# Single-tile groups at both ends of a fused block's second part, and a new planned order

## The chip, the cores and the metric

The kernel runs on one core of a Trainium2 chip. The core has five engines that work in parallel, each on its own queue of instructions in a fixed order: TensorE (PE in the profile, with its weight loads as PEld), VectorE (DVE), ScalarE (ACT), GpSimd (POOL) and SyncE (SP, which here only starts transfers). The metric is device time in microseconds, lower is better; before and after are compared by the medians of repeated runs on the same chip.

## What is computed

One block of a network on 2048 positions and 640 channels, in bfloat16. First a mixer: a short and a long convolution over positions (the long one as a Fourier transform of length 4096), gated by a normalized copy of the input. Then an MLP with a shift of channel groups along the positions. Six modulation vectors come from `c`.

```python
mod = (_silu(c) @ w_mod).reshape(c.shape[0], 6, 1, -1)     # sa, ca, ga, sb, cb, gb
h = _layernorm(x) * (1 + ca) + sa
x = x + ga * _A_ref(h, A_k, A_v, A_shift_k, A_ssm_k, A_ssm_D)
h = _layernorm(x) * (1 + cb) + sb
x = x + gb * _B_ref(h, B_w1, B_w2, B_w3, B_w4)

def _A_ref(q, k, v, shift_k, ssm_k, ssm_D):
    ...                                   # k_shift: 4-tap convolution of k
    kv = k_shift * v
    ...                                   # y: kv convolved with ssm_k, by FFT
    return q * (y + kv * ssm_D)

def _B_ref(x, w1, w2, w3, w4):
    h = _gelu(_layernorm(x) @ w1)         # w1: 640 x 640
    ...                                   # four groups of channels shifted by +1, -1, +2, -2
    x1 = x + hs                           # hs = shifted h @ w2, 640 x 640
    return x1 + _gelu(_layernorm(x1) @ w3) @ w4   # w3: 640 x 1728, w4: 1728 x 640
```

## The kernel before

The 2048 positions are 16 tiles of 128. The first part does the transforms: `stage1` and `stage2` for the filter and for the product k_shift * v, then `inverse1` (ten blocks of spectral products, `TA` and `TB` on DVE at L605, each with a half-swap of the filter's spectrum by two DMAs, L601, one from SP and one from POOL) and `inverse2` (L657, 512 small matmuls in six groups of tiles). In the first part DVE and ACT mostly evict PSUM (L208, L210). The modulation vectors (`mod_half`, L482) are made beside it.

The second part goes tile by tile through a long chain:

- `chain_a`: gate and first residual (L714, L717, with the row sum as a by-product), the sum of squares on ACT (`square_sum`, L706), `ln_finish` (mean, variance, root);
- `chain_b`: norm (L580 on ACT or L582 on DVE), times 1 + cb (L728), plus sb (L729), squares, `ln_finish`;
- `chain_c`: norm and `turn`, which transposes the tile, on PE (L747, with a copy at L753 or L755) for the first groups, by a DMA of SP (L740) for the rest;
- `mm_w1`: W1 and its GELU (L794, L796 and, for the fifth block of channels, L804, L810). The shift by one or two positions is a shift of 32 or 64 columns in the buffer `gsf`, as positions are strewn over tiles; at the first and last tile small copies (L817 to L833) make the wrap-around;
- `mm_w2`: W2 (L849), second residual (L857), squares, `ln_finish`, norm and `turn`;
- `mm_w3`: W3 in four pieces (named f0, f4, f8, f12 below) and GELU (L882, L886);
- `mm_w4`: W4 (L928, and L934 for the last half block), final residual (L951, L956, L957) and the stores. The last tile has its own ending, `last_tile`.

`ln_finish` (L687) makes, for a group of two tiles, the negative mean and the part of the variance that comes from it on POOL or DVE (L692 to L694), then on POOL the variance, its power -0.5 and the product of the two (L699, L700, L701).

All of it is done in pairs of tiles: `chain_a` to `mm_w1` for tiles (0, 1), (2, 3) and so on, `mm_w2` to `mm_w4` for (1, 2), (3, 4) up to (15, 0). `spare` adds, in four groups of `mm_w4`, a DVE transpose (L896 to L902) and a POOL operation (L908 to L914) on a buffer that is no longer used.

The order of the work is not left to the program's loops. Each step is a task with a number, an engine, and its reads and writes; the string `ORDER` at the top lists the tasks in the order in which they are issued, with the engine and the PSUM places chosen. It was made beforehand by a planner that works with the costs in the `add` calls; the kernel only replays it. So each engine runs its tasks in the order of the string.

Of the kernel before, what the change touches and what calls it, by code (L numbers as in the profile page):

```python
# [16 lines left out]
P = 128  # L17
# [9 lines left out]
0S 18D 2S 19G 36G 56G 21G 20D 23D 24A 22D 25A 27G 28D 29D 31A 37G 68G 69D 30A 32D 26G 84P:0 85A 90P:1 88P:2 91A 89A 4S 72G 73D 106P:3 107A 3S 70G 50G  # L27
71D 102P:0 103D 38G 39G 104P:1 105A 6S 86P:2 87D 40A 49G 96P:3 97A 92P:0 93A 94P:1 8S 118P:2 5S 74G 95A 75D 1S 66G 98P:3 99A 41G 112P:0 113A 116P:1 9S
119D 67D 114P:2 108P:3 42G 43G 51D 44A 53A 117D 115A 10S 122P:0 110P:1 52D 11S 123D 109A 34S 100P:2 101D 54A 33S 57G 82P:3 78P:0 79D 201S 111A 45G 83A
55G 80P:1 76P:2 253D 47S 120P:3 81A 77A 170P:0 171A 121D 46S 194P:1 195A 178P:2 179A 198P:0 35S 144P:1 145A 199D 142P:3 143D 188P:2 189A 176P:0 177D  # L30
202S 182P:1 183A 48S 140P:3 141A 180P:2 181D 148P:0 149A 156P:1 164P:3 165A 157D 138P:2 139D 190P:0 136P:1 137D 191A 162P:3 163A 200S 174P:2 175A 12S
172P:0 173D 196P:1 197A 152P:3 153D 13S 160P:2 203S 168P:0 169D 7S 146P:1 161A 147A 186P:3 187D 154P:2 166P:0 155A 167D 58G 59G 192P:1 193A 150P:3
151A 60A 61G 258P:2 158P:0 159A 254D 184P:1 185A 259D 213A 208A 126P:3 127D 272P:0 273A 266P:1 267D 124P:2 125D 270P:3 271A 209D 214A 14S 130P:1
262P:2 263A 65G 219S 220P:0 221A 255D 15S 128P:3 16S 131D 260P:2 129D 17S 62G 63G 64A 222S 261A 264P:0 265A 211A 210D 256D 132P:1 274P:3 275A 276P:2
277A 225S 134P:0 133D 268P:3 269A 135D 223P:1 224A 288P:2 289A 212G 489D 280P:0 281A 282P:3 283A 226P:1 284P:2 257D 290P:0 227D 291A 228S 285D 231S
234S 205S 286P:1 287D 278P:3 279A 480D 292P:2 232P:0 251G 296P:1 293A 233D 252S 294P:3 247G 486D 297D 229P:0 230D 235P:2 236D 362S 295A 298P:3 299A
249G 316P:1 360P:0 317D 361A 304P:2 305D 350P:3 351A 346P:1 347A 300P:0 301D 332P:2 333A 238G 354P:3 355D 312P:1 313A 302P:0 303D 340P:2 341A 243S
318P:3 319D 358P:1 359A 336P:0 337A 386S 342P:2 248G 308P:3 343D 237S 310P:1 244S 311D 330P:0 309A 331A 352P:2 353D 314P:3 315A 306P:1 322P:0 323A
326P:2 327A 334P:3 307D 335D 338P:1 339A 250G 320P:0 324P:2 325A 344P:3 242G 348P:1 349A 321D 328P:0 245S 241G 240S 356P:2 345D 329D 357A 364D 363G
365D 366P:3 367A 370S 368P:1 481D 239S 246G 372D 369A 371G 387G 373D 374P:0 375A 376P:2 377A 216A 378S 380D 379G 381D 442S 443P:3 382P:1 395G 383A  # L40
384P:0 389D 385A 388D 394S 397D 396D 392P:2 483A 393A 390P:1 404D 215G 398P:0 400P:2 401A 399A 403G 402S 405D 444D 408P:3 412D 406P:2 445S 409A 407A
411G 410S 413D 416P:0 417A 419G 414P:3 415A 446P:2 420D 418S 421D 422P:0 454S 424P:3 428D 427G 391A 426S 435G 429D 423A 434S 455P:1 456A 436D 432P:0
433A 447D 437D 430P:1 431A 451S 452P:2 487D 453A 490D 491D 438P:0 440P:1 439A 457S 458P:2 441A 459A 448S 449P:0 450A 425D 501G 217D 479G 492D 475S
493D 484D 485D 482D 495P:31 496A 497A 519D 520D 218G 522D 498P:20 523D 473S 499D 204S 500A 521A 525G 488D 474S 543D 476S 524A 557D 526G 554D 558D
502P:31 504A 503A 555D 531D 559A 556A 508P:02 509A 510A 511P:13 544D 532D 494D 527D 528D 533D 534A 529D 530A 505P:02 513A 206S 512A 560G 561G 566A
562D 602D 535G 536G 545D 605D 477S 563D 606D 540D 541P:3 472S 537D 607A 538P:1 603D 539D 567D 568D 542A 478G 551P:3 546D 564D 608G 604A 609G 610D 207S
578A 570D 506D 514S 549P:1 569A 565A 571G 572D 575D 611D 552A 614A 573P:0 574D 576P:3 577D 586P:0 550A 615D 584P:1 616D 617A 612D 613A 553G 587A 618D
619G 579D 580D 547D 515S 548D 672D 585A 620D 621P:3 623D 624P:0 625A 675D 676D 677A 591P:1 673D 674A 678G 592D 588P:0 622A 634P:3 632P:1 679G 680D
589D 593A 635A 684D 685D 681D 682D 686D 688D 594G 590A 633A 595G 596D 599D 636P:0 637D 518G 600P:3 597P:1 601D 598D 507A 639P:2 656P:0 463A 687A 640D
642D 683A 638A 689G 690D 692A 641A 643G 657A 693S 461D 652P:3 653A 654P:1 644D 460D 645P:2 646D 647A 648P:0 464D 691S 702P:3 649D 703A 700P:2 701A  # L50
724P:0 462G 469D 650P:3 626A 581D 582D 583D 740D 741D 742A 517S 465G 651A 725A 655A 704P:2 705D 470D 471G 466A 627D 628D 743D 718P:3 707P:0 708D 719A
710G 709A 629D 630D 744D 765A 746G 745A 747G 722P:2 723A 720P:1 706A 631D 516S 658P:30 467D 748A 749D 750D 711G 715D 712D 713P:2 468G 721A 752D 751A
716P:1 717A 659P 714D 790P:2 786P:1 753D 754D 756G 755A 757G 694A 791A 806D 807D 695D 666D 696D 787A 809D 766D 758D 726P:02 759S 660D 760D 761S 770P:3
810D 811A 768P:1 808A 812G 661D 771A 769A 784P:3 667D 772P:1 813G 814D 815D 818D 816D 697D 819D 698D 817A 866G 820D 828A 822D 728D 773D 762A 699D 871D
829D 775P:0 788P:1 727P 821A 823G 662S 824D 825S 785A 826A 827S 833P:3 776D 763D 777A 789A 665S 764D 872D 778G 664S 874D 875D 774A 831P:0 734D 792P:12
834A 832A 835P:3 836D 838P:0 779G 668S 780A 781S 928G 782A 839D 783S 853P:3 854A 663S 735D 669S 841G 840A 830D 837A 842G 936D 843A 877G 844S 729D 794D
845A 847P:0 849P:3 876A 767D 933D 873A 934D 846S 935A 937D 939D 671S 878G 731S 850A 851P:1 736S 938A 670S 852A 883D 732S 884D 885D 940G 793P 915P:3
848A 886A 733S 800D 911P:1 879D 880D 881D 887D 916A 855P:02 941D 942D 909P:3 795D 857D 913P:0 945A 946D 739S 797S 882A 796S 943D 888G 947D 949D 889A
890S 738S 730S 798S 912A 891A 892S 910A 737S 948A 895P:1 944A 950G 953A 951D 952S 799S 954S 896A 858D 893P:3 894A 801D 856P 863D 914A 897P:1 898D 899A
900P:3 957P:0 958A 901D 902A 955P:2 956A 903G 805S 904G 907D 908S 917P:13 959G 865D 960P:0 961D 999P:2 963P:0 1000D 905A 964D 966G 965A 906S 864D  # L60
996P:2 997D 860S 802S 919D 972P:0 1002D 1001A 962A 978P:2 979A 974P:1 976P:2 977A 868S 918P 975A 998A 804S 927D 967G 970D 968D 803S 920D 973A 969S
1003G 862S 925D 971S 1014P:2 1012P:1 1015A 1006A 861S 1013A 1010P:0 1004D 859S 980P:32 870S 921S 1007S 1005S 1038P:1 981P 1039A 926D 982D 1008P:3 990D
930S 869S 988D 867S 983D 984S 986S 985S 1009A 1026D 922S 1032P:1 1033A 924S 923S 989D 992S 994S 1034P:2 1011A 1016P:31 1035A 932S 1036P:0 995S 931S
929S 1018D 1019D 1021S 1037A 1022S 1020S 1017P 1024D 1023S 987S 1025D 1030S 1028S 1049D 1040P:230 1041P 1043D 993S 1044D 1029S 1031S 1045S 1048S 1046S
1050D 1051D 1052D 1054S 1053S 1056S 1055S 1042P 1057D 1058D 1059S 1047S 1061S 991G 1027G 1060A 1062A
# [3 lines left out]
class Task:  # L69
    __slots__ = ("no", "eng", "cost", "fn", "deps", "lat", "alloc", "frees", "succ", "on", "kb", "rate", "port", "act")  # L70
# [10 lines left out]
class Planner:  # L81
# [9 lines left out]
    def add(self, eng, cost, fn, r=(), w=(), lat=0.0, alloc=None, use=None, after=(), kb=0.0, rate=330.0, port=0.0, act=1.0):  # L91
        t = Task()
        t.no = len(self.tasks)
        t.eng, t.cost, t.fn, t.lat, t.kb, t.rate, t.port, t.act = eng, cost, fn, lat, kb, rate, port, act
# [43 lines left out]
def kernel(  # L138
# [259 lines left out]
    def stage1(xL, xkey, b, h, what):  # L398
        dstv = T1h[h].rearrange("p k (b q r) -> p k b q r", b=ND, q=4)
        for qd in range(2):  # L400
            ps = Slot()

            def f(e, ps=ps, qd=qd):
                psv = pst(ps, name="ps_s1")[:].rearrange("p b (j x) -> p (b j) x", j=2)
                for ml in range(4):
                    s0 = b * 2048 + 64 * (16 * h + 8 * qd + 2 * ml)
                    nc.tensor.matmul(psv[:, ml, :], lhsT=xL[:, s0:s0 + P], rhs=F1r, start=True, stop=True)  # L407
            add("PE", 0.44, f, r=[(xkey, 2048 * b, 2048 * b + 2048), ("F1", 0, 1)], alloc=ps)
            evac(dstv[:, :, b, :, 4 * qd:4 * qd + 4],
                 lambda t: t[:].rearrange("p b (j x) -> p (b j) x", j=2).rearrange("p m (q k) -> p k q m", q=4),  # L410
                 1024, ps, [("T01", 10240 * h, 10240 * h + 10240, ("s1", what))])
            pl.tasks[-1].deps.add(pl.tasks[-2])
            pl.tasks[-2].succ.append(pl.tasks[-1])
# [368 lines left out]
    def gk(g):  # L782
        return ("gs", g, g + 1, "gs")
# [270 lines left out]
```

## Time and profile before

| | |
|---|---|
| median of 9 runs | 313.7 us |
| lowest, highest | 312.29, 317.83 us |
| the profiled execution: its time | 313.01 us |
| its span, first to last instruction | 311.3 us |
| mean granted TensorE clock | 0.952 |
| busy: PE, DVE, ACT, POOL | 271.9, 233.4, 206.5, 117.7 us |
| chain that ended last: PE, ACT, DMA, POOL, DVE | 51%, 16%, 9%, 8%, 7% of the span |

The profile is of one execution. Its 40 slices are 7.8 us each. "PEclk" is the clock that TensorE was granted, in tenths. A row of a timeline has start, length, engine, line, operation and tile; what stands in brackets is the idle time before it and who ended it. "issue" means that nothing which the profile shows was waited for. The first part ends at about 104 us and the second part's last matmul ends at 306.1 us.

### The profile page before, as it was taken

Reading aid. Unit: us, or ns where it says so; the run is one execution under the profiler, and the core shown is the slowest. Engines: PE = TensorE matmul, PEld = TensorE weight load, DVE = VectorE, ACT = ScalarE, POOL = GpSimd, SP = SyncE. Lnnn points to the kernel's source line nnn. Section 1 sums busy time; section 2 is a strip of 40 time slices with the busy share of each in tenths; the row PEclk is TensorE's granted clock in tenths of the full one; section 3 lists DMA queues with packets and bytes.
Section 4 is the critical chain, followed back from the end, with each engine's and each line's share of the span. In section 5 each row is a group of like instructions: output and inputs, shape, how many; then the busy total and the mean of one; then the engine's idle time right before and its main releaser. Section 6 shows DMA issues by size and latency. Waiting matters only on the chain.

```text
span 311.3 us, 7171 instructions
## 1 busy us (share of the span) xinstructions
PE 271.9 (87%) x2816; PEld 204.6 (66%) x2816; DVE 233.4 (75%) x436; ACT 206.5 (66%) x339; POOL 117.7 (38%) x254
## 2 busy tenths in 40 slices
PE   0999999996959655668999999999999999999993
PEld 0665555764958543446788777678877768878762
DVE  8999999999979988897686698817773367554243
ACT  4889999995868668978968757653968513703300
POOL 5977083251810456445343743413411112610000
PEclk9999999999899955788999999999999999999998
DMA  6998999696999922920020011211423041221111
GB/s 205 273 209 203 203 218 239 169 241 149 259 217 257 279 55 67 395 101 2 15 53 0 2 21 28 51 34 29 78 47 76 9 55 42 55 47 34 36 46 47
DMA packets 56849, 35.39 MB, mean 114 GB/s; under 512 B 38528, under 2 KB 53504, under 8 KB 56816
## 3 DMA queue, kind: packets, MB, share of 16 engines
q1 hardware_dynamic: 55632, 31.68, 43.4%
q0 software_dynamic: 1088, 3.21, 4.5%
q8 instruction: 22, 0.36, 0.5%
q14 instruction: 11, 0.09, 0.1%
q10 hardware_dynamic: 96, 0.04, 0.1%
HBM read 16.31 MB, written 2.62 MB: 61 GB/s over the span
## 4 chain that ended last, share of the span: by engine, by line
PE 51%; ACT 16%; DMA 9%; POOL 8%; DVE 7%; issue 6%; SPq 1%; ACTq 0%; DVEq 0%; POOLq 0%
PE ps_w L928 16%; PE ps_w L882 16%; PE ps_w L849 6%; DMA RK<-R 4%; ACT R L208 4%; ACT RG L706 3%; PE ps_w L794 3%; ACT T L208 3%; DMA Ra<-in_A_ssm_k_dram 2%; PE ps_s L424 2%; DMA RG<-RG 2%; PE ps_mod L482 2%; ACT Rb L208 1%; PE ps_i L657 1%; DVE R L729 1%
## 5 line engine op out<-in xcount | busy, mean ns | idle before, releaser
L882 PE MATMUL ps_w<-R,T 128*128 128x256 bf16 x560 | 63.6, 273 | 0.0
L882 PEld LDWEIGHTS <-T 128*128 128x128 bf16 x560 | 54.5, 98 | 7.6 <-issue 0.8
L928 PE MATMUL ps_w<-T,R 128*128 128x320 bf16 x416 | 59.0, 299 | 0.0
L886 ACT ACTIVATE R<-ps_w 128x1024 bf16<-128x1024 f32 (+1 forms) x32 | 28.5, 911 | 34.3 <-PE ps_w L882 24.4
L928 PEld LDWEIGHTS <-R 128*128 128x128 bf16 x416 | 40.6, 98 | 15.2 <-issue 0.3
L706 ACT ACTIVATE RG<-R 128x640 bf16<-128x640 bf16 x32 | 23.5, 735 | 14.4 <-DVE R L857 11.8
L951 DVE TENSOR_TENSOR T<-ps_w,R 128x640 bf16<-128x640 f32 x15 | 12.3, 823 | 27.2 <-PE ps_w L928 16.2
L208 ACT CAST T<-ps_s 128x1024 bf16<-128x1024 f32 x31 | 29.3, 1027 | 2.6 <-PE ps_s L407 2.5
L407 PE MATMUL ps_s<-F1bd,Rb 128*128 128x256 bf16 x160 | 22.4, 289 | 8.3 <-DVE Rb L394 8.0
L849 PE MATMUL ps_w<-RG,R 128*128 128x320 bf16 x160 | 24.7, 309 | 1.8 <-ACT R L796 1.2
L407 PEld LDWEIGHTS <-Rb 128*128 128x128 bf16 x160 | 16.3, 104 | 14.3 <-DVE Rb L394 8.4
L857 DVE SCALAR_TENSOR_TENSOR R<-ps_w,R 128x640 bf16<-128x640 f32 x16 | 13.2, 822 | 16.4 <-PE ps_w L849 16.4
L616 PE MATMUL ps_i<-EA,Rb 128*128 128x128 bf16 x160 | 20.8, 228 | 5.3 <-DVE modv L493 2.6
L208 ACT CAST R<-ps_s 128x640 bf16<-128x640 f32 x38 | 24.1, 718 | 1.4 <-PE ps_s L424 1.3
L208 ACT CAST T<-ps_i 128x1024 bf16<-128x1024 f32 x19 | 18.3, 1015 | 8.8 <-PE ps_i L617 8.6
L424 PE MATMUL ps_s<-T,RG 64*128 64x320 bf16 x256 | 22.0, 297 | 0.9 <-DMA RG<-RG 0.4
L699 POOL TENSOR_TENSOR lnv<-stat,lnv 128x2 f32<-128x2 f32 x24 | 6.7, 277 | 42.0 <-ACT RG L706 40.5
L849 PEld LDWEIGHTS <-R 128*128 128x128 bf16 x160 | 15.8, 101 | 9.0 <-ACT R L796 1.5
L617 PE MATMUL ps_i<-EB,Rb 128*128 128x128 bf16 x160 | 20.7, 228 | 1.2 <-DVE Rb L605 1.2
L210 DVE CAST R<-ps_s 128x640 bf16<-128x640 f32 x26 | 19.9, 819 | 0.7 <-PE ps_s L424 0.3
L794 PE MATMUL ps_w<-R,RG 128*128 128x256 bf16 x160 | 19.5, 279 | 0.2 <-ACT R L796 0.2
L617 PEld LDWEIGHTS <-Rb 128*128 128x128 bf16 x160 | 16.4, 103 | 4.9 <-issue 3.2
(173 smaller groups left out, 543.0 us busy)
## 6 DMA issues: line engine op xcount, KB each, us to landing
Ra<-in_A_ssm_k_dram SPq DMA_DIRECT2D x5, 512.0 KB, 4.7
Ra<-in_A_q_dram SPq DMA_DIRECT2D x8, 320.0 KB, 5.1
R<-in_w_mod_dram SPq DMA_DIRECT2D x6, 400.0 KB, 7.8
out_dram<-RH SPq DMA_DIRECT2D x60, 40.0 KB, 1.6
T<-in_B_w_dram SPq DMA_DIRECT2D x1, 2160.0 KB, 9.4
T<-in_B_w_dram SPq DMA_DIRECT2D x1, 2080.0 KB, 14.5
RH<-in_w_mod_dram SPq DMA_DIRECT2D x4, 400.0 KB, 4.7
RK<-R POOLq DMA_DIRECT2D x5, 256.0 KB, 6.8
```

What stands on the lines that cost most here:

```text
L208: nc.scalar.copy(dst, src(ps.tile))
L210: nc.vector.tensor_copy(dst, src(ps.tile))
L407: nc.tensor.matmul(psv[:, ml, :], lhsT=xL[:, s0:s0 + P], rhs=F1r, start=True, stop=True)
L424: nc.tensor.matmul(psv[:, g], lhsT=Gs[p, k, 64 - 64 * cc:192 - 64 * cc], rhs=T1b[p, cc * 32 + k], start=(cc == 0), stop=(cc == 1), tile_po ...
L616: nc.tensor.matmul(psv[:, w, :], lhsT=Av[:, r_, :, g_], rhs=EAf, start=True, stop=False)
L617: nc.tensor.matmul(psv[:, w, :], lhsT=Bv[:, r_, :, g_], rhs=EBf, start=False, stop=True)
L706: add("ACT", 0.74, lambda e: nc.scalar.activation(junk, src, ACT.Square, scale=float(D) ** -0.5, accum_out=stat[:, li, 1, t:t + 1]), r=[sk ...
L794: nc.tensor.matmul(pt[:, fb, :], lhsT=w1_sb[:, b, 160 * fb:160 * fb + P], rhs=hT[:, b, :], start=(b == 0), stop=(b == ND - 1))
L849: nc.tensor.matmul(pt[:, hf, 0:320], lhsT=gsf[:, fb, c0:c0 + P], rhs=w2_sb[:, fb, 320 * hf:320 * hf + 320], start=(fb == 0), stop=(fb == 4))
L882: nc.tensor.matmul(pt[:, fl, :], lhsT=w3_sb[:, b, fb * P:(fb + 1) * P], rhs=xT[:, b, :], start=(b == 0), stop=(b == ND - 1))
L886: nc.scalar.activation(g3[g % 2][:, f0:f0 + fn, :], ps.tile[:, 0:fn, :], ACT.Gelu_apprx_tanh)
L928: nc.tensor.matmul(pts[i][hf][:, hf, 0:320], lhsT=gg[:, fb, i * P:(i + 1) * P], rhs=w4_sb[:, fb, 320 * hf:320 * hf + 320], start=(fb == 0 ...
```

## The change

- The groups: `CG` = tile 0, 1, 2 singly, then pairs (3, 4) to (13, 14), then 15 singly, for `chain_a` to `mm_w1`. `MG` = tile 1 singly, pairs (2, 3) to (14, 15), then tile 0 singly, for `mm_w2` to `mm_w4`.
- `ln_finish` has a short form for a single tile, and a "quick" form that leaves out the product L701. With "quick" (tiles 0 to 2; W2 groups 0 and 1), `chain_b` makes (x - mean) * (1 + cb) before the root is known and multiplies by the root in the step that adds sb; the other norms are (x - mean) * root on DVE.
- Accesses are declared by single tile: W2 of tile t reads W1's tiles t-1 to t+1 and its edge, no more whole pairs.
- W2 and W4 go over the block of the contraction outside and the two halves of the output inside. `inverse2` takes its first five tiles as (0, 1, 2), (3, 4).
- PE transposes: for tiles 0 to 4 before W1 (0 to 5 before), for tiles 1 to 5 before W3 (1 to 6 before).
- `spare` is gone. `ORDER` is new, from a planner that also counts PE's instructions (`ni`) in blocks of 256.

```diff
-        nm, rs, nb = (lnv[:, 8 * li + t0 // 2, j, :] for j in range(3))
+        nm, rs, nb = (lnv[:, 3 * li + j, t0:t0 + n] for j in range(3))
...
+            if n == 1:
+                eng_of[e].tensor_scalar(rs, nm, nm, EPS, ALU.mult, ALU.subtract)
+            else:
+                eng_of[e].tensor_tensor(rs, nm, nm, ALU.mult)
+                eng_of[e].tensor_scalar(rs, rs, -1.0, EPS, ALU.mult, ALU.add)
...
+            if n == 1:
+                nc.gpsimd.tensor_tensor(rs, s2, rs, ALU.subtract)
+            else:
+                nc.gpsimd.tensor_tensor(rs, s2, rs, ALU.add)
             nc.gpsimd.tensor_tensor(rs, rs, mhalf[:, 0:n], ALU.pow)
-            nc.gpsimd.tensor_tensor(nb, nm, rs, ALU.mult)
+            if not quick:
+                nc.gpsimd.tensor_tensor(nb, nm, rs, ALU.mult)
...
+    def normed(dst, dk, src, sk, rn, i):
+        rs, nb, lk, nm, nk, quick = rn
+        if quick:
+            return add("DVE", 0.44, lambda e: nc.vector.tensor_scalar(dst, src, nm[:, i:i + 1], rs[:, i:i + 1], ALU.add, ALU.mult),
+                       r=[sk, lk], w=[dk], port=0.8)
+        return norm(dst, src, rs[:, i:i + 1], nb[:, i:i + 1], [sk, lk], dk)
...
+            if quick:
+                add("DVE", 0.82, lambda e, u=u, A=A, i=i: nc.vector.scalar_tensor_tensor(
+                    u, x_all[:, A, :], nm[:, i:i + 1], cb1, ALU.add, ALU.mult), r=[xk_(A), nk, ("modB", 6, 12)], w=[uk], port=0.8)
...
+                h_all[:, A, :], u, rs[:, i:i + 1] if quick else 1.0, sbv, ALU.mult, ALU.add, accum_out=stat[:, 1, 0, A:A + 1]),
...
-                for hf in range(2):
-                    for fb in range(5):
+                for fb in range(5):
+                    for hf in range(2):
...
-            lo, hi = (t * 4 - 2) // 8, (t * 4 + 5) // 8
-            r = [("gs", max(0, lo), min(7, hi) + 1)]
+            r = [("gs", max(0, t - 1), min(NT, t + 2)), ("gx", t + 1, t + 2)]
```

Read out of the two strings, the places of the order that matter here (a number is a tile; "swap 5" is the half-swap of spectral block 5):

```
PE, from the end of inverse1
before: inverse2 (0,1) (2,3,4) (5,6,7) (11,12,13) (14,15) (8,9,10); transposes 1, 0; W1 (0,1); 2, 3; W1 (2,3);
        4, 5; W2 2, 1; W1 (4,5); W2 3; transposes 2, 1; W2 4; W3 (1,2) f12, f4, f8; ...
after:  inverse2 (0,1,2); two modulation products; (3,4) (14,15) (5,6,7) (8,9,10); transpose 0; (11,12,13); W1 0;
        transposes 1, 2; W1 1; W1 2; transposes 3, 4; W2 1; W1 (3,4); transpose 1; W2 2, 3; W3 1 f0, f4, f8;
        W1 (5,6); transpose 3; W3 1 f12; transpose 2; W2 5, 4; W3 (2,3) f12, f0, f4; transposes 5, 4; W4 1; ...
ACT, from the evictions of inverse2
before: (0,1) both halves; one half of (2,3,4); squares a0, a1; (5,6,7) both; a3, a2; (11,12,13) both; b1, b0; ...
after:  one half of (0,1,2); modulation; norm for q5; (3,4) both; a0; (14,15) both; a2, a1; b0; a4; (5,6,7) both;
        one half of (8,9,10); a3; copy of transpose 0; b2, b1; ...
POOL
before: swaps 0, 1, 3, 2, 4; LayerNorm-1 finish 4, 5; swaps 5 to 9; ... finish of LayerNorm 2 for (2,3); edge copies of
        tile 0; finish for (4,5); ... pad copy of W3 after the first finish of W2's group
after:  swaps 0, 1, 3, 2, 4 to 9; LayerNorm-1 finishes 4 and 6; ... edge copies of tile 0 after the finish of the
        last statistics (14, 15); pad copy of W3 after LayerNorm 2 of (5,6)
SP
before: ... last modulation load; W2; inputs 8 to 15 among them; W1; W3; W4; DMA transposes 7, 6; halves of W4's rest
after:  ... last modulation load; W1; W2; inputs 8 to 15 among them; one half of W4's rest; W3; DMA transposes 5, 6; W4; ...
```

## The prediction

> **What bounds the kernel now.** I read the 40 slices first, then the busy time by stretch, then TensorE's and VectorE's timelines of the seam between the two parts, last the chain of waits.
>
> ```profile
> PE   0999999996959655668999999999999999999993
> PEclk9999999999899955788999999999999999999998
> ```
>
> A slice is 7.8 us. TensorE (PE) is full from slice 19 on; in slices 14 to 18 (109 to 148 us) it is half busy at half to 0.8 clock. The view by stretch gives the sizes:
>
> ```profile
> 105.00:151.10 46.10, 29.44 (x658) 20.96 (x636) 39.65 (x99) 36.79 (x72) 24.79 (x63) 0.74 0.41 128
> 151.10:306.10 155.00, 153.23 (x1275) 120.61 (x1272) 93.70 (x203) 82.14 (x143) 44.81 (x105) 1.00 0.19 39
> ```
>
> The columns are the length, the busy time of PE, its weight loads, VectorE (DVE), ScalarE (ACT) and GpSimd (POOL), then clock, DMA share and GB/s. From 151.1 to 306.1 us PE is busy 153.2 of 155.0 us at full clock. Its pieces in the chain confirm that this is work:
>
> ```profile
> 257.01 7.64 PE ps_w L882 x70
> 264.65 3.53 PE ps_w L928 x26
> ...
> 277.17 0.38 PE ps_w L934 x4
> ```
>
> W3: 8 x 7.64 = 61.1; W4: 16 x 3.53 + 8 x 0.38 = 59.5; 12 W2 tiles at 1.36 = 16.3; five W1 groups at 2.18 + 0.55 = 13.7; 20 transposes, 1.1. Sum 151.7 of 155.0, so 3.3 us are gaps. The end is therefore set by when PE gets saturated and what it has done by then. The seam:
>
> ```profile
> 104.70 1.41 PE L657 MATMUL ps_i<-T,RH 32*32 32x160 bf16 x114
> 109.00 2.10 PE L657 MATMUL ps_i<-T,RH 32*32 32x160 bf16 x128 [2.89 <-issue]
> 113.55 2.08 PE L657 MATMUL ps_i<-T,RH 32*32 32x160 bf16 x126 [2.45 <-issue]
> ...
> 125.53 1.23 PE L804 MATMUL ps_w1x<-R,RG 128*128 128x256 bf16 x5 [0.67 <-DVE R L755]
> ...
> 139.29 4.04 PE L849 MATMUL ps_w<-RG,R 128*128 128x320 bf16 x20
> ...
> 151.09 5.62 PE L882 MATMUL ps_w<-R,T 128*128 128x256 bf16 x50
> ```
>
> The 512 small matmuls of the inverse stop with no releaser after 114, then after another 128: 128 matmuls with 128 weight loads are 256 instructions, the block in which PE's program arrives. Blocks begin at 109.00, 113.55, 117.0 and 120.7 us. Then W1 starts at 125.5, W2 at 139.3, W3 at 151.1: that ramp is what the change attacks. In the chain there is one more loss before it:
>
> ```profile
> 76.77 0.51 POOL RG L601
> ...
> 80.02 1.54 POOL rs L548
> ...
> 83.28 0.51 POOL RK L601
> 83.90 7.05 DMA RK<-R
> ```
>
> A half-swap of the spectrum waits on POOL's queue behind a LayerNorm finish (L545 to L550, 77.3 to 82.8).
>
> **The change, part by part.** All sums are against the profiled execution: span 311.3 us, time 313.0 (1.7 around it). The median shown is 313.7, 0.7 more.
>
> *Matmul work.* Single-tile groups replace 70 W3 matmuls and 50 W1 matmuls of 256 columns by 140 and 100 of 128. A 256-column one advances 7.64/70 = 0.109 us. For 128 columns with a new weight each, the inverse's rows start 0.055 to 0.06 apart:
>
> ```profile
> 96.86 0.22 PE L616 MATMUL ps_i<-EA,Rb 128*128 128x128 bf16 x1
> 96.92 0.22 PE L617 MATMUL ps_i<-EB,Rb 128*128 128x128 bf16 x1
> ```
>
> At 0.0557 this costs 240 x 0.0557 - 120 x 0.109 = +0.3 us. [...] W2 and W4 with the halves inside the block loop keep count and shape: 0, bounds -1 to +1 as the trace has no such alternation between banks.
>
> *Scale product ahead of the root* (tiles 0 to 2, W2 groups 0 and 1). POOL drops L701 (0.20) and, for one tile, the mean's step at L693/L694 shrinks by one instruction. After the root, norm 0.36, product 0.41, sum 0.75 become one sum of 0.75: 0.8 us off each of three serial passes. The new u (a tensor-and-two-operand form) costs 0.75 by row L729, against 0.77 for the pair it replaces: DVE's load is unchanged. These norms may not go to ACT any more; DVE is 86% busy here (39.65 of 46.1), counted in the walk below.
>
> *Finer accesses.* W2 of tile 1 needs tiles 0 to 2 instead of 0 to 3. The edge copies (L817 to L822, 133.6 to 135.9) leave POOL's path: before, they hold up the finish of LayerNorm 2 for tiles 4, 5; after, they sit behind the last statistics. Worth about 2.3 us there, inside the walk.
>
> *Spare work.* Four DVE transposes (L896 to L902: 1.95, 1.95, 1.24, 1.24) and four POOL operations (4.06 for the longest) go. They run at 249 to 287 us under continuous PE work: 0. If that cover were gone, a W4 eviction behind the 3.89 us norm at 268.96 would count.
>
> *The seam, walked* with the durations of before (STT 0.83 with its accumulator read, tensor-tensor 0.41, norm 0.36 to 0.4, ACT square 0.93, root and subtraction on POOL 0.9, evictions 0.6 to 0.95). Between the last spectral product and the first a-product, DVE has 5.9 us of work (5.8 before), so both start from 107.0. The block border falls ten matmuls later, since two modulation products now follow the first inverse group: all 96 matmuls of tiles 0 to 2 pass, then 10, then 18 of tiles 3, 4. ACT's first square stands behind the evictions of 3, 4, which need the block of 109.0: square done 111.9, root 112.9, h of tile 0 113.7. Then two evictions and two squares, its square 115.9, root 116.9, norm 117.3. PE's transpose of tile 0 sits behind inverse groups in the block of 117.0: 118. ACT copies it after four evictions or squares, 121.0. W1 of tile 0 starts at 121.0 (125.5 before). Tiles 1, 2 follow DVE's order: copies 125.9 and 127.5, W1 of tile 2 done at 130 at half clock, W2 of tile 1 at 131.3 (139.3 before), W1 of 3, 4 done 136, W3 of tile 1 at 140.4 (151.1 before). Tiles 5, 6 now cross by DMA (2.6 us), norms 140.3 and 141.5, W1 144.2 to 146.9.
>
> At 147.9 PE has done W1 for seven tiles (9.6), W2 for three (4.1), W3 for one (3.9): 17.6 of 164.5 (21.9 + 21.8 + 61.3 + 59.5). With 1.1 of transposes, 148.0 are left. With the same 3.3 us of gaps the last matmul ends at 299.2, 6.9 us earlier. The walk lets nothing stretch; before, norms stand at 0.58 for 0.4 and roots at 1.18 for 0.7 in just this stretch. I keep 4.
>
> [...]
>
> *Order of the first part.* DVE and ACT are over 95% busy from 20 to 60 us; moving evictions between them leaves both sums within 2 us. Here POOL issues all swaps ahead of that LayerNorm finish: the 2.31 us that DVE stands still before 90.16 can go. But DMA is full from 75 to 104 us (over 0.9 in nearly all slices), and the weights W1, W2 come in the same stretch. Bounds -3 to +4; I take -1.
>
> *Queues.* On SP, the W4 load moves behind the DMA transposes of tiles 5, 6; issued at 121.8 before, now at about 144. It took 14.5 us together with W3; the W3 load took 9.4. Landing 153.5 to 158.5; PE reaches W4 at about 158: 0. W3's pad copy stands behind LayerNorm 2 of tiles 5, 6 on POOL (about 140.4), level with W3's start: 0.
>
> *End.* The last group has W3 hidden behind the W4 of tile 15. From the last matmul to the end 5.2 us stay.
>
> Sum: -4 -1 +0.3, about -4.7: span 306.6, time 308.3, with the 0.7 **309 us**.
>
> **Rivals.**
> 1. *A ramp that is hidden anyway* (14%): each stall moves to the next queue entry; in-order ACT and the instruction blocks hold W1 where it was. For: the block intervals of 3.5 to 4.6 us remain, 512 small matmuls still come nearly in a row. Against: W2 no longer needs tile 3. Time 311 to 316, centre 313.5.
> 2. *Slower: the W4 load on SP* (19%). It waits for the norm of tile 6 and two transposes. If that norm comes at t, W4 lands at up to t + 17.6 (two issues of 1.3, 0.5, 14.5), against PE's 158. At t = 141.5 it costs 1; at t = 151 it costs 10.6, and all PE work behind it waits in order. With the gain of 4.7 the balance turns at t = 145, and passes 1% slower at 148.3. Price at 151: 309 + 10.6 = 319.6. For: t hangs on LayerNorm 2, DVE, POOL and ACT in turn. Against: w4 alone on the queue should come in 9.4. A first part at its +4 adds to it.
> 3. *Both gains whole* (12%): the walk's 6.9 and 3 in the first part: 303.5.
> [...]
>
> **How the numbers follow.** My forecast (55%) spans 305 to 312, most of it under 310.5; own range 305 to 312. A measurement here tells about 1% (3.1 us) from no change, and single runs spread from 312.3 to 317.8. Faster by over 1%: 12 + 50 = 62%; within: 5 + 14 = 19%; slower: 19%. The range 303 to 317 leaves out some 4% below and 15% above.
>
> **What would show it.** First W2 near 131 and first W3 near 140 us; TensorE saturated from about 148; matmuls of 128 columns in W3 0.056 apart; no wait of the swap on POOL at 77 to 83; the last matmul near 301. I am wrong if PE has gaps of more than 4 us in total after 150, above all before the first W4, or if the inverse starts after 106.

## The result, and the profile after

| | before | after |
|---|---|---|
| median | 313.13 us (43 runs) | 309.61 us (14 runs) |
| lowest, highest | 311.0, 317.87 us | 307.41, 311.68 us |
| profiled execution: time, span | 313.01, 311.3 us | 309.77, 307.8 us |
| last matmul ends | 306.12 us | 301.92 us |

The ratio is 0.9901 with a 95% interval of 0.9881 to 0.9921: 3.1 us less, 2.5 to 3.7, against a forecast of 309 from 313.7. The median of before counts 14 of its 43 runs that lie apart from the others, between 315.9 and 317.9 us, while every ratio here rests on the others alone.

The slices of after (7.7 us each):

```profile
PE   0998999996889937877999989999999999999992
PEclk9999999999799955699999999999999999999999
```

TensorE is full from slice 19 on, as before. In the slices ahead of that it is busier: 7 to 8 tenths from slice 15 on, not 5 to 8, and the clock is back at 0.9 or more in slice 17, not 19.

By stretch (length, busy time of PE, its weight loads, DVE, ACT, POOL, then clock, DMA share and GB/s):

```profile
103.00:149.30 46.30, 33.95 (x773) 27.02 (x763) 38.12 (x100) 39.48 (x87) 29.87 (x72) 0.78 0.44 121
149.30:301.90 152.60, 150.72 (x1291) 117.86 (x1288) 81.31 (x194) 82.86 (x150) 36.64 (x103) 1.00 0.23 47
```

The seam is as long as before, but TensorE is busy for 34.0 us of it instead of 29.4 (1.5 of the 34.0 are a modulation product that before makes ahead of the inverse). The stretch behind it is 152.6 instead of 155.0 us, with gaps of 1.9 us. TensorE's timeline of the seam:

```profile
102.87 1.21 PE L658 MATMUL ps_i<-T,RH 32*32 32x160 bf16 x96
...
112.83 2.10 PE L658 MATMUL ps_i<-T,RH 32*32 32x160 bf16 x128 [3.63 <-issue]
116.56 1.00 PE L658 MATMUL ps_i<-T,RH 32*32 32x160 bf16 x46 [1.63 <-issue]
...
121.05 2.31 PE L815 MATMUL ps_w<-R,RG 128*128 128x128 bf16 x20
...
131.96 1.52 PE L870 MATMUL ps_w<-RG,R 128*128 128x320 bf16 x10
...
141.07 3.51 PE L904 MATMUL ps_w<-R,T 128*128 128x128 bf16 x60
146.29 0.70 PE L825 MATMUL ps_w1x<-R,RG 128*128 128x256 bf16 x5 [1.71 <-DMA R<-RK]
...
159.04 3.69 PE L934 MATMUL ps_w<-T,R 128*128 128x320 bf16 x26
```

The inverse starts 1.8 us earlier, W1 4.5, W2 7.3, W3 10.0 and W4 14.2 us earlier than before. An earlier first piece is not the same gain at the end: the first pieces are small now, and TensorE still waits between them. The lead at the end is 4.2 us. Sixty matmuls of 128 columns take 3.51 us, and TensorE waits 1.71 us for a DMA transpose of tiles 5, 6. W4 waits for nothing.

### The profile page after: what moved, and what is told of

It is laid out like the page before. It is cut to its first block, busy times and chain, and to the rows that moved or that the text cites. A ratio compares the mean times of both kernels' runs of the same rounds, so it can differ in the third digit from the quotient of the medians.

```text
span 307.8 us, 7417 instructions
## 1 busy us (share of the span) xinstructions
PE 273.1 (89%) x2926; PEld 206.3 (67%) x2926; DVE 218.9 (71%) x430; ACT 210.2 (68%) x359; POOL 116.1 (38%) x257
## 3 DMA queue, kind: packets, MB, share of 16 engines
q0 software_dynamic: 1136, 3.41, 4.0%
## 4 chain that ended last, share of the span: by engine, by line
PE 47%; issue 11%; DVE 11%; DMA 10%; ACT 9%; POOL 8%; SPq 2%; POOLq 0%; ACTq 0%; DVEq 0%
PE ps_w L904 12%; PE ps_w L934 10%; PE ps_s L425 5%; PE ps_w L870 4%; PE ps_s L408 4%; PE ps_ksh L457 4%; DMA R<-RK 3%; PE ps_w L815 3%; ACT RG L726 3%; DMA RG<-R 3%; POOL lnv L712 2%; DMA RH<-RK 2%; DVE Rb L395 2%; SPq L966 2%; DMA Ra<-in_A_ssm_k_dram 1%
## 5 line engine op out<-in xcount | busy, mean ns | idle before, releaser
L904 PE MATMUL ps_w<-R,T 128*128 128x256 bf16 (+1 forms) x630 | 64.0, 261 | 0.0
L904 PEld LDWEIGHTS <-T 128*128 128x128 bf16 x630 | 55.8, 98 | 7.4 <-issue 1.1
L934 PEld LDWEIGHTS <-R 128*128 128x128 bf16 x416 | 40.3, 98 | 15.4 <-issue 0.3
L908 ACT ACTIVATE R<-ps_w 128x1024 bf16<-128x1024 f32 (+2 forms) x36 | 28.9, 826 | 28.6 <-PE ps_w L904 28.5
L209 ACT CAST T<-ps_s 128x1024 bf16<-128x1024 f32 x33 | 31.6, 1025 | 3.6 <-PE ps_s L408 3.6
L408 PEld LDWEIGHTS <-Rb 128*128 128x128 bf16 x160 | 16.6, 106 | 15.2 <-DVE Rb L395 9.2
L209 ACT CAST R<-ps_s 128x640 bf16<-128x640 f32 x37 | 23.4, 723 | 1.9 <-PE ps_s L425 1.8
L870 PE MATMUL ps_w<-RG,R 128*128 128x320 bf16 x160 | 23.1, 299 | 0.0
L712 POOL TENSOR_TENSOR lnv<-lnv,mhalf 128x2 f32<-128x2 f32 (+1 forms) x29 | 21.9, 757 | 2.3
L618 PE MATMUL ps_i<-EB,Rb 128*128 128x128 bf16 x160 | 20.5, 228 | 1.6 <-DVE Rb L606 1.6
L815 PE MATMUL ps_w<-R,RG 128*128 128x256 bf16 (+1 forms) x200 | 21.1, 270 | 0.0
L815 PEld LDWEIGHTS <-RG 128*128 128x128 bf16 x200 | 18.3, 108 | 1.6 <-issue 0.3
```

Source lines behind the costliest of these rows:

```text
L209: nc.scalar.copy(dst, src(ps.tile))
L712: nc.gpsimd.tensor_tensor(rs, rs, mhalf[:, 0:n], ALU.pow)
L815: nc.tensor.matmul(pt[:, fb, 0:cw], lhsT=w1_sb[:, b, 160 * fb:160 * fb + P], rhs=hT[:, b, 0:cw], start=(b == 0), stop=(b == ND - 1))
L870: nc.tensor.matmul(pt[:, hf, 0:320], lhsT=gsf[:, fb, c0:c0 + P], rhs=w2_sb[:, fb, 320 * hf:320 * hf + 320], start=(fb == 0), stop=(fb == 4))
L904: nc.tensor.matmul(pt[:, fl, 0:cw], lhsT=w3_sb[:, b, fb * P:(fb + 1) * P], rhs=xT[:, b, 0:cw], start=(b == 0), stop=(b == ND - 1))
L908: nc.scalar.activation(g3[g % 2][:, f0:f0 + fn, 0:cw], ps.tile[:, 0:fn, 0:cw], ACT.Gelu_apprx_tanh)
```

## The experiments

The kernels were timed in three series, each on another chip and each beside before on that chip (medians of before 313.13, 312.66, 312.92 us). The first series has the four edits of before that come first, the second the four edits of after behind them, the third the rest. The edits of ORDER move words of the string; what each word is stands with it.

**Before, spare work left out** (`spare` adds its two tasks with empty bodies: four DVE transposes and four POOL operations whose results nobody reads).

> The kernel before, with the four spare DVE transposes and four spare POOL operations left out (they feed nothing). Theory A (the gain is won before TensorE is saturated, at the seam): they run at 249 to 287 us under continuous matmuls, so 0 +- 0.5 us, last matmul still near 306. Rival B (the gain is DVE and POOL load taken away): most of the 3.5 us, ratio near 0.99.

Measured: 315.77 us, ratio 1.0048 [0.9998, 1.0098]. No gain to be seen; but its 12 runs spread from 311.8 to 317.3 us, so a gain of a microsecond could hide. The profiled run (314.02 us) lost time ahead of all spare work: the first part is that of before, yet its spectral products took 27.5 us from the first to the last (before 25.9), the swap behind the LayerNorm finish was issued at 85.59 us (before 83.28), and the inverse began at 107.51 (before 104.70). The same edit follows below on a base with that finish moved.

**Before, the LayerNorm finish moved behind the swaps.** 215G is the finish L545 to L550 for tiles 4 and 5, 435G the last half-swap.

```diff
-390P:1 404D 215G 398P:0
+390P:1 404D 398P:0
...
-426S 435G 429D
+426S 435G 215G 429D
```

> The kernel before with one task moved: the LayerNorm-1 finish of tiles 4 and 5 behind the last half-swap on POOL, as after has it. Theory A: DVE's wait before the spectral product of block 5 (2.3 us) goes, inverse2 starts 1.5 to 2 us earlier than 104.7, and as the seam is serial the last matmul follows by 1 to 2 us (ratio 0.994 to 0.997). Rival C (hidden anyway: DMA is full from 75 to 104 us, or the instruction blocks hold the seam): inverse2 starts at most 0.5 us earlier, or earlier with the end unchanged; ratio 1.000.

Measured: 311.46 us (310.36 to 312.85), ratio 0.9949 [0.992, 0.9977], and no run above 312.9. POOL's queue in this run:

```profile
82.35 0.51 POOL L601 DMA_DIRECT2D RK<-R  x1 [2.47 <-DVE Rb L605]
83.48 0.51 POOL L601 DMA_DIRECT2D Rb<-R  x1 [0.62 <-DVE Rb L605]
85.80 0.51 POOL L601 DMA_DIRECT2D RG<-R  x1 [1.80 <-DVE Rb L605]
```

In before, a swap was issued at 76.77 and the next only at 83.28, behind the finish. Now POOL waits for the products instead. DVE's timeline, before (first row) and this run (second row):

```profile
90.16 1.23 DVE L605 TENSOR_TENSOR Rb<-R,RK 128x2048 bf16<-128x2048 bf16 x1 [2.31 <-PE ps_i L617]
```

```profile
87.69 1.22 DVE L605 TENSOR_TENSOR Rb<-R,RK 128x2048 bf16<-128x2048 bf16 x1
```

The stand of 2.31 us is gone, and the inverse begins at 102.46 instead of 104.70 us. One word of ORDER is worth about 1.6 us (0.7 to 2.5).

**Before, edge copies moved back.** The copies at the left edge (553G) go behind LayerNorm 1 of tiles 8, 9 (747G). For this their stated access to the W1 output is replaced by a dependence on its Gelu.

```diff
-612D 613A 553G 587A
+612D 613A 587A
...
-745A 747G 722P:2
+745A 747G 553G 722P:2
```

> The kernel before with the edge copies of tile 0 (2.3 us on POOL at 133.6) moved behind LayerNorm 1 of tiles 8, 9, their read of tile 0's GELU declared finer so that the order allows it. Theory A: LayerNorm 2 of tiles 4, 5 ends up to 2 us earlier, W2 starts at 137 to 138 instead of 139.3, the end 1 to 2 us earlier (ratio 0.994 to 0.997). Rival C: W1 of 2, 3 and its GELU are the bound there, the POOL wait turns into another one; W2 at 139, ratio 1.000.

Measured: 315.5 us (312.26 to 319.18), ratio 1.0019 [0.9973, 1.0065]. From the inverse to the first W2 it took 34.3 us, before 34.6: the POOL path that the prediction priced at 2.3 us was worth 0.3 in the trace, and nothing in the times. The finish of LayerNorm 2 that stood behind the copies starts 31.2 us behind the inverse in both traces; without the copies, POOL waits there for ACT's square.

**Both moves in before.**

> The two moves together, on the kernel before with its pairs. Theory A: they add up, 2 to 4 us, ratio 0.987 to 0.994; what then remains to after is the single-tile groups and the quick norms. Rival C: no more than one of them alone. If this equals after (0.990), the single tiles bring nothing.

Measured: 311.8 us, ratio 0.9965 [0.9932, 0.9998]: no more than the swaps alone.

**After, the finish put back among the swaps** (215G between 395G and 403G, half-swaps 4 and 5).

```diff
-445S 456A 215G 495P:10
+445S 456A 495P:10
...
-391A 395G 397D
+391A 395G 215G 397D
```

> The changed kernel with the LayerNorm-1 finish of tiles 4 and 5 put back between the half-swaps of blocks 4 and 5 on POOL. Theory A: inverse2 starts 1.5 to 2 us later than 102.9 and the end follows by 1 to 2 us (ratio to before 0.993 to 0.997 instead of 0.990). Rival C: unchanged, 0.990.

Measured: 310.38 us, ratio 0.9903 [0.9864, 0.9942]. A loss is not shown: it lies 0.8 us above after by medians of two series, and 1.1 us above the two edits of its own series that changed nothing (309.33 and 309.21, below), but its ratio is that of after in the first measurement (0.9901). The trace does not decide it: the products took 24.7 us from the first to the last, 23.4 in the profile of after, but 25.1 when after was profiled again.

**After without the quick norms.**

```diff
-    quick_c, quick_m = 3, 2
+    quick_c, quick_m = 0, 0
```

ORDER's numbers follow; each quick sum becomes a norm and a product in the same place.

> The changed kernel without the quick norms: tiles 0 to 2 and W2 groups 0 and 1 take the root times mean on POOL, norm, product and sum as all others. Theory A: about 0.8 us on each of three serial passes, of which one or two lie on the path: W2 of tile 1 starts 1 to 2 us later than 132.0, the end 0.5 to 2 us later (0.992 to 0.996). Rival D (the norms may go to ACT again, and DVE's load is the same, so it is nothing): 0.990 +- 0.001.

Measured: 309.33 us, ratio 0.9872 [0.9823, 0.9922], not slower than after. W2 of tile 1 comes 29.7 us behind the inverse's start, in after 29.1: 0.6 us on the path, nothing to be seen at the end. The norms that the prediction called "0.8 us off each of three serial passes" are not worth a measurable time.

**After, edge copies early** (539G, the left edge, just ahead of LayerNorm 2 of tiles 3, 4).

> The changed kernel with the edge copies of tile 0 put early on POOL, just ahead of LayerNorm 2 of tiles 3, 4. Theory A: that finish comes about 2 us later than 130.5, W1 of 3, 4 likewise, W3 of tile 1 one to two us after 141.1, the end 1 to 2 us later (0.993 to 0.997). Rival C: 0.990, the wait is taken up before W1 of 5, 6.

Measured: 310.61 us (307.92 to 312.31), ratio 0.9938 [0.9905, 0.9972]. About 1 us above after by the medians, 1.3 above the two edits of the same series that changed nothing; the intervals meet. W2 of tile 1 comes 30.1 us behind the inverse's start, in after 29.1.

**After with the old loops** (halves outside, blocks inside, in W2 and W4).

```diff
-                for fb in range(5):
-                    for hf in range(2):
+                for hf in range(2):
+                    for fb in range(5):
```

> The changed kernel with the loops of W2 and W4 as before: half of the output outside, block of the contraction inside. Both theories: 0 +- 0.5 us, ratio 0.990; more than 1 us would mean that alternating between two PSUM banks costs or saves something the sum had at nothing.

Measured: 309.21 us, ratio 0.9866 [0.9823, 0.9909]: the loop order costs and brings nothing that the times show.

**After once more**, as the measure of the third series.

> The changed kernel once more, unedited, as the measure for the three others of this call: 309.6 us within 0.4 by every theory, W2 of tile 1 at 132 and W3 of tile 1 at 141 us.

Measured: 308.77 us, ratio 0.9868 [0.9829, 0.9907], twice the 0.4 us allowed away from 309.6. The ramp moved as well: W2 of tile 1 at 133.73 and W3 at 142.73 us, since its inverse began 1.8 us later (104.64). Its end came only 0.9 us later. Differences below 1 us between kernels of different series mean little.

**After, W2 of tile 1 late.** 580P (W2 of tile 1) goes behind W1 of tiles 3, 4; its residual (581D) and square (582A) behind those of tile 6.

```diff
-611D 580P:1 608D 620P:3 581D 582A 618P:2 621A
+611D 608D 620P:3 618P:2 580P:1 621A
...
-665D 666A 659D
+665D 581D 666A 582A 659D
```

> After, with W2 of tile 1 (and its residual and square) moved behind W1 of tiles 3 and 4, about where accesses by pairs would have put it: W2 of tile 1 at 136.9 instead of 132.0. Theory A, the earlier start of the block chain (W2 of a single tile as soon as its own neighbours are there) is what the ramp gains: its norm and so W3 of tile 1 come at 144 to 145 instead of 141, the time is 2 to 3 us longer, 311.6 to 312.6. Theory B, TensorE has other work to put in front and the ramp is limited by DVE: W3 moves, but W1 of tiles 5 and 6 fills the hole; at most 0.8 us longer, up to 310.4.

Measured: 314.65 us, ratio 1.0055 [1.0024, 1.0087]; 5.9 us more than after in the same series, twice the largest figure expected. TensorE's timeline:

```profile
133.98 1.25 PE L825 MATMUL ps_w1x<-R,RG 128*128 128x256 bf16 x5 [1.80 <-DVE R L777]
135.03 3.48 PE L815 MATMUL ps_w<-R,RG 128*128 128x256 bf16 x20
138.35 1.52 PE L870 MATMUL ps_w<-RG,R 128*128 128x320 bf16 x10
143.26 0.45 PE L769 MATMUL ps_tr<-RG,RH 128*128 128x128 bf16 x5 [3.40 <-DVE RH L721]
143.55 4.55 PE L870 MATMUL ps_w<-RG,R 128*128 128x320 bf16 x20
147.94 3.51 PE L904 MATMUL ps_w<-R,T 128*128 128x128 bf16 x60
```

And its stretches of 2 us:

```profile
132.00:134.00 2.00, 0.20 (x5) 0.03 (x3) 1.89 (x7) 1.94 (x5) 0.98 (x5) 0.98 0.00 0
134.00:136.00 2.00, 2.00 (x10) 1.44 (x11) 1.09 (x3) 1.80 (x6) 0.73 (x2) 0.50 0.03 8
136.00:138.00 2.00, 2.00 (x14) 1.52 (x13) 0.68 (x2) 0.78 (x3) 0.00 (x0) 0.67 0.00 0
...
144.00:146.00 2.00, 2.00 (x10) 1.18 (x9) 1.86 (x8) 1.43 (x4) 0.45 (x2) 0.54 0.00 0
146.00:148.00 2.00, 2.00 (x11) 1.19 (x10) 1.35 (x5) 1.53 (x4) 1.03 (x3) 0.61 0.00 0
```

In after, W2 of tile 1 filled the pause between two serial passes. Without it, TensorE waits 1.80 and 3.40 us, and each wait is followed by some 3.4 us at half clock: the twenty W1 matmuls take 3.48 instead of 2.35 us and the twenty of W2 4.55 instead of 2.88. (A mean of 0.67 between half and full is two thirds of the stretch at half: 2.0 + 1.3 us in the first dip, and by 0.54 and 0.61, 1.8 + 1.6 us in the second.) So the price of a wait was the wait and 1.1 to 1.7 us more. From the start of the inverse to the last matmul this run took 204.2 us, after in the same series 198.2: the 6.0 us lie behind the start of the inverse, and this ramp shows where. In the 3.41 us ahead of each dip TensorE was not idle, but busy for 21% and 27%. The edit is not a true pair-wise kernel, for the rest of the order was planned with W2 in its early place: DVE, too, stood 3.29 us for the late W2's residual. So 6 us is what the early W2 is worth in this order, not what single tiles bring over pairs.

**After with TensorE transposes for tiles 5, 6.**

```diff
-    pe_c, pe_m = 4, 3
+    pe_c, pe_m = 5, 3
```

In ORDER the two DMA transposes become PE transposes behind the second piece of W3 of tile 1, their copies go to ACT and DVE, and the residual of tile 3 comes ahead of the statistics; the PSUM tags behind that are renamed.

> After, with the transposes of normed tiles 5 and 6 on TensorE (ten more 128x128 matmuls and two evictions) in place of the two DMA transposes for which TensorE waited 1.71 us. Theory A, that wait is on the path: W1 of tiles 5 and 6 begins at about 145.0 in place of 146.3, and with 0.6 us of work added the time is 0.5 to 1.0 us shorter, 308.6 to 309.1. Theory B, the two transposes and the evictions on DVE and ACT push the norm of tiles 2 and 3 and the hole opens there: no change, or up to 0.5 us longer.

Measured: 308.86 us, ratio 0.9878 [0.9836, 0.992]; after in the same series 308.77. Its timeline:

```profile
142.15 0.72 PE L769 MATMUL ps_tr<-RG,RK 128*128 128x128 bf16 x10
...
143.94 0.71 PE L825 MATMUL ps_w1x<-R,RG 128*128 128x256 bf16 x5
...
147.65 0.45 PE L769 MATMUL ps_tr<-RG,RH 128*128 128x128 bf16 x5 [0.81 <-DVE RH L721]
...
158.17 0.73 PE L769 MATMUL ps_tr<-RG,RH 128*128 128x128 bf16 x10 [0.66 <-ACT RH L581]
```

The wait of 1.71 us is gone, and W1 of 5, 6 starts 2.35 us earlier than in after (1.0 of it from an earlier run of everything). But 0.81 and 0.66 us come back as waits for the norms of the next transposes, and ten matmuls are added. The time lies in the range of theory A, but that range was set against 309.6; beside 308.77 there is no gain to be seen. Taking the wait away saved nothing, since the next waits, for DVE and ACT, took its place.

**Before, swaps moved and spare work left out.**

> Before, with the first-part finish moved behind the last table load as in the earlier run, and the spare operations of DVE and POOL left out as well (they compute nothing that is used). Theory A, spare work is beside the path in a stage that TensorE bounds: the same as with the move alone, 311.5 within 0.5. Theory B, they hold up the DVE and POOL queues of the second part: 1 to 2 us less, about 310.

Measured: 309.93 us (308.94 to 311.2), ratio 0.9897 [0.9858, 0.9935], against 0.9949 with the move alone: 1.5 us by the medians, across two series, where the intervals overlap but neither holds the other's ratio. The traces show what of it is the spare work. With it (rows of DVE, POOL and PE):

```profile
187.76 1.50 DVE L582 TENSOR_SCALAR R<-Ra,lnv 128x640 bf16<-128x640 bf16 x1 [1.37 <-POOL lnv L701]
...
193.29 0.82 DVE L951 TENSOR_TENSOR T<-ps_w,R 128x640 bf16<-128x640 f32 x1
```

```profile
187.68 1.40 POOL L908 TENSOR_TENSOR Rb<-Rb,modv 128x640 bf16<-128x640 bf16 x1
```

```profile
187.16 0.72 PE L804 MATMUL ps_w1x<-R,RG 128*128 128x256 bf16 x5
...
192.08 1.52 PE L849 MATMUL ps_w<-RG,R 128*128 128x320 bf16 x10
194.16 1.52 PE L849 MATMUL ps_w<-RG,R 128*128 128x320 bf16 x10 [0.56 <-DVE T L951]
...
300.93 3.71 PE L928 MATMUL ps_w<-T,R 128*128 128x320 bf16 x26
```

Without it (DVE, PE):

```profile
186.78 0.45 DVE L582 TENSOR_SCALAR R<-Ra,lnv 128x640 bf16<-128x640 bf16 x1 [1.36 <-POOL lnv L701]
...
191.27 0.82 DVE L933 TENSOR_TENSOR T<-ps_w,R 128x640 bf16<-128x640 f32 x1
```

```profile
186.18 0.72 PE L804 MATMUL ps_w1x<-R,RG 128*128 128x256 bf16 x5
...
191.10 2.88 PE L849 MATMUL ps_w<-RG,R 128*128 128x320 bf16 x20
...
299.24 3.71 PE L910 MATMUL ps_w<-T,R 128*128 128x320 bf16 x26
```

A norm of 0.45 us starts 0.08 us behind POOL's spare product and ends 0.18 us behind it, 1.05 us late. An eviction further on in DVE's queue (L951; L933 in the kernel without spare work) is late by that: it starts 6.1 instead of 5.1 us behind the start of the W1 piece (L804). TensorE stands 0.56 us for its PSUM; without spare, both tiles of W2 run in one row. The profile of before has the same three rows (1.40 us at 189.12 on POOL, 1.49 at 189.20 on DVE, a wait of 0.57 at 195.61 on PE), and in the first run without spare work TensorE has no such wait either. In before, a later norm shows the same: started at 268.96 behind a POOL product of 4.06 us (268.61), it took 3.89 us and ended 0.18 us behind it. Why the norm takes so long beside the product, the traces do not show.

From the start of that W1 piece to the end of the last matmul it takes 117.5 us in the four profiles with spare work (before, the swaps moved, the edge copies moved, both) and 116.8 in the two without: 0.7 us, the whole of it at this wait, for the second tile of W2 starts 2.08 us behind the first instead of 1.36. From the last matmul to the end it takes 5.1 to 5.2 us with spare work and 4.9 without, for a reason that the traces do not show. So the traces put the spare work at 1.0 us. The other 0.5 of the 1.5 cannot be its work, for no spare operation has run ahead of that piece; it is of the size by which after moved between two series.

One thing ahead of that piece looks like a difference between the two traces and is not one. In the profile with spare work, as in that of before, the twenty W2 matmuls behind the wait of 2.3 us take 4.55 and 4.04 us, in the other four profiles of before and its edits 2.88. In these traces the clock changed at steps of 3.41 us; by such steps, with the swaps moved (first two rows) and with the edge copies moved (last two):

```profile
134.73:138.14 3.41, 1.46 (x16) 1.16 (x17) 3.22 (x7) 2.39 (x4) 1.30 (x2) 1.00 0.00 0
138.14:141.55 3.41, 3.41 (x15) 1.97 (x13) 1.76 (x7) 3.05 (x8) 1.72 (x6) 0.50 0.00 0
```

```profile
135.82:139.23 3.41, 1.58 (x17) 1.26 (x18) 3.22 (x9) 2.43 (x4) 1.21 (x2) 1.00 0.00 0
139.23:142.64 3.41, 2.96 (x25) 2.18 (x23) 1.67 (x5) 3.24 (x8) 1.71 (x6) 1.00 0.02 5
```

All six traces wait alike there. What differs is how much of the wait falls into one step: the clock fell behind steps that were busy for 32% (before) and 43% (swaps moved), and did not behind 44% (both moves), 46% (edge copies), 57% and 60% (the two without spare work).

## Why the prediction was right, and where it was not

The forecast of 309 was right to 0.6 us. Its gain of 4.7 us was counted from 313.7; measured were 3.1 and, in the third series, 4.1. The division of it was not right: one term, the spare work, was put at nothing and was not nothing, and the ramp was made too large.

*Matmul work, "+0.3 us"*: it stood. W3's sixty take 3.51 us; less the last one's own length, 0.22 by the rows of single matmuls, that is 0.056 each, as taken from the inverse's rows.

*The ramp, "I keep 4".* The walk named the places well: W1 at 121.0, found 121.05; W2 131.3, found 131.96; W3 140.4, found 141.07; the first W4 at about 158, found 159.04. That is partly luck: the walk had the stall of the instruction blocks after 124 matmuls; in this profile it came later, for 3.63 us after 252 (96, 10 and 146), and the root of tile 0 ended 2.6 us behind its square, in the walk 1.0. The walk also held half clock up to W1 of tiles 3, 4, since it read full clock in before only from about 141; but twenty W1 matmuls at 133.57 there took 2.34 us, which is full clock, and the half clock behind them was a second dip. In after the clock was full from 129.0, and W1 of 3, 4 took 2.35 us. The errors cancelled. Behind the walk, 1.7 us were lost to the DMA transpose of tiles 5, 6, which the walk had landing at 144.2. What the walk had done at 147.9 (W1 of seven tiles, W2 of three, W3 of one) was done at 149.9, and its last matmul, at 299.2 before the ramp was cut from 6.9 to 4 us, came at 301.9. (The 3.3 us of gaps in that sum are a remainder; the trace of before has 1.8, after 1.9, and the term drops out.)

What the ramp is worth shows against before without its spare work. From the inverse to the last matmul its two profiles take 200.5 us (with 20.5 us of half clock in the seam) and 199.8 (with 17.1); the two of after take 199.1 (20.5) and 198.2 (17.1). Like with like, that is 1.4 and 1.7 us. At the end after loses part of it: from the last matmul to the end it takes 5.9 and 5.6 us, those two 4.9, where the prediction had "5.2 us stay". In the third series the medians of before with both losses taken out and of after are 1.2 us apart. So the term of 4 is nearer to 1, and its interval reaches zero. Of its parts, quick norms and edge copies were sized at 0.8 us for each of three passes and at 2.3 within the walk, and measured at nothing to 1. The early W2 of a single tile is what the new order cannot do without: it fills a pause between two serial passes, and taken away from the finished order it costs 5.9 us, more than the whole gain.

*Order of the first part, "I take -1"*: it stands. Moving one word in before gave -1.6 (-0.7 to -2.5), with the mechanism as predicted: the finish on POOL between two swaps, and 2.31 us of DVE that go. Within after the same move could not be told from noise.

*"Spare work ... They run at 249 to 287 us under continuous PE work: 0"*: this step failed. Two of the eight operations run earlier, the first on POOL at 189 and the second at 203 us, and the first meets a DVE norm on which an eviction and TensorE wait: 0.7 us there and 0.3 at the end, 1.0 us in the traces, where the sum had nothing. So luck has its part in the total: 3 us too much for the ramp stand against 1.6 too little for the first part and the spare work, and the rest of the miss went unseen, since the forecast was counted from 313.7 and the measured ratio from 312.7 (309.61 / 0.9901).

*The rivals.* The W4 load was issued at 144.8 and 145.4 us and W4 did not wait: the norm of tile 6 came at 142.75, 2.3 us short of the turning point at 145. The ramp that is hidden anyway was half true: the seam is still 46 us long, and block stalls of 3.63, 1.63 and 0.65 us remain. Gaps behind 150 us sum to 1.9 us, below the 4 that would have refuted the forecast. (Rival 3 should have been 304.1 by its own terms: 313.7 less 6.9 and 3, plus 0.3.)

Open: what makes the times of before spread so far (311.0 to 317.9 us), and why they spread no more (310.4 to 312.9) once that finish had left its place among the swaps. The swap issued late in the run of 314.02 us, above, points at that queue; no profile is of a run above 315 us. Open, too, is why after takes longer from the last matmul to the end.

## What to carry to other kernels

Take a kernel's change apart with the small edits first: one LayerNorm finish ahead of DMA issues on a queue, and work whose results nobody reads, made 1.6 and 1.0 us of the 3 to 4 us that a rebuilt ramp seemed to bring. Work "beside the path" has to be looked up operation by operation, with what the other engines run at that time: a DVE norm beside a POOL product took 1.50 us here instead of 0.45. In a ramp, fill the pauses between serial passes with whatever TensorE can do: two pauses of 1.80 and 3.40 us cost their length here and, at half clock behind them, 1.1 and 1.7 us more.

## What the runs showed of the hardware

- The clock of TensorE changed in steps of 3.41 us: in all fourteen traces each stretch at half clock that ends ahead of the last matmul lasted a whole number of them. From 122 to 153 us it fell seven times, each time behind a step in which TensorE was busy for 21 to 43%, and never behind one with 44% or more; ahead of that it also fell behind fuller steps, at 108.54 us in after behind one that was busy for 80%. Half clock ended only behind steps busy for 79% or more (36 times), and lasted on behind some that were busy for up to 83%.
- In the seam the clock is at half for 14 to 24 us in every kernel, dips included, although TensorE is busy for 34.0 of the 46.3 us in after. It differs between executions of one kernel: 20.5 us in the first profile of after, 17.1 in the second.
- TensorE's program arrived in blocks of 256 instructions, by these counts: the queue of instructions named q8 moved 22 packets in before, where TensorE has 2816 matmuls and 2816 weight loads (22 times 256), and 23 in after, for 2926 of each (22.9 times 256). In the four stalls of the inverse of before without a releaser, TensorE goes on 1.4 us behind the end of such a packet (ends at 107.58, 112.11, 115.61, 119.29 us; starts at 109.00, 113.55, 117.00, 120.73). The two rows of the pages, before and after:

```profile
q8 instruction: 22, 0.36, 0.5%
```

```profile
q8 instruction: 23, 0.38, 0.5%
```

- The block stalls differ from run to run: 3.63, 1.63 and 0.65 us in one execution of after, 0.97 (after 124 matmuls, as in the walk), 1.79 and 1.36 in another, up to 4.64 in edits of before. The end moves less than that: W1 of tile 0, counted from the inverse, came after 18.2 us in the one and 17.2 us in the other.
- A DVE norm that started 0.08 us behind a POOL product of 1.40 us took 1.50 us instead of 0.45 (the swaps moved, with and without spare work).
